# Attention output turned by float32 transposes and a 16-column product instead of one 144-column product

## The chip, the core and the metric

The kernel runs on one core of a Trainium2 chip. The metric is the device time of one execution in microseconds (us). TensorE (PE in the profile, with its weight loads as PEld) multiplies: it holds one operand as weights, up to 128 x 128, and streams the other past it, column by column. VectorE (DVE), ScalarE (ACT) and GpSimd (POOL) do the rest, SyncE (SP) issues most of the DMA transfers.

## The reference

Three stages follow each other: attention with a position bias, a layer of eight experts of which each token takes one, and a dense layer with a gate.

```python
scores = scale * np.matmul(q, k.transpose(0, 1, 3, 2)) + bias      # 4 batches, 8 heads, 576 tokens, 64 wide
attn = softmax(scores)                                             # divisor: sum + 1e-9
x = (attn @ v).transpose(0, 2, 1, 3).reshape(2304, 512)
logits = x @ w_gate + modality_bias[modality_id]                   # 8 experts
e_idx = argmax(logits);  gate_w = softmax(logits)[e_idx]
out[mask_e] = gate_w * (relu(x[mask_e] @ w1[e]) @ w2[e])           # e = 0..7
h = out @ w_in;  result = (h * sigmoid(1.702 * h)) @ w_out
```

The change lies at the end of attention, where `x` and its share of `logits` are made.

## The kernel before

Attention goes over 16 groups `g`: a pair of heads `hp` (4 of them) times a batch `b` (4). The 576 tokens of a group are four blocks of 128 rows and a last one of 64 rows; the last block holds both heads one above the other. That makes 80 units. A unit has its scores (`sc`, L571, float32r, 288 columns), which DVE joins with the bias (L574) and ACT exponentiates (L578). TensorE turns the result `p` by float32 transposes (`tp`, L599 and L612; `tp_r`, L607 and L618), ACT and DVE copy it out as `pt`.

Then comes the product with v (`pv`), in two parts for each group: part 0 has the first 256 tokens, part 1 the other 320 (256 and the last 64). Group 15 is cut into three, with part 2 of 256 and part 3 of the last 64 tokens alone. A part begins with one product in the form of the whole array (L646), after which each head has four products (L652) whose weights are 64 columns wide: head 0 in columns 0 to 63 of the array, head 1 in columns 64 to 127. The result has the head's width down the partitions and tokens along the row; ACT copies it to `xt` (L656).

`xs()` makes from it tokens down the partitions. The weights are 128 tokens of `xt`, and what streams past is `rh`, 144 columns: for each of the two heads 64 columns of the identity matrix and 8 columns of `w_gate`. So one product gives the turned x and the logits together (L673). For the last 64 tokens of a group the weights have 64 columns (L676). A float32 product that isn't a transpose shows in the trace as two passes, each with its own weight load; a transpose as one. DVE divides by the row sums: `Lp` (L692) takes the logits, `xo` (L708, L714) the x, and SP stores `xo` to `X`.

The kernel's text is not the order in which the engines work: a scheduler arranges the instructions of each engine as the program is built, and TensorE runs its products in the order written there. How many transposes, score products and pieces of `pv` stand beside each other is decided by it. After attention come the routing (a serial chain over DVE and TensorE), the experts and the dense layer.

Of the kernel before, what the change touches and what calls it, by code (L numbers as in the profile page):

```python
# [15 lines left out]
ALU = mybir.AluOpType  # L16
# [3 lines left out]
B, H, S, D = 4, 8, 576, 64  # L20
HP = H // 2
FH = 32
E, DM, FE = 8, 512, 1024
# [22 lines left out]
REST = (12, 12, 17, 17)  # L46
# [67 lines left out]
def body(ctx, tc, qk, vv, few, mid, ew1, ew2, ww, cst, alog, out, dbg=None):  # L114
    nc = tc.nc
    pe, act, dve, pool, sp = nc.tensor, nc.scalar, nc.vector, nc.gpsimd, nc.sync
    stop = dbg["stop"] if dbg else None

    biasD = tc.dram_tile([36 * TROWS + IROW], F32, name="biasD")
    X = dbg["X"] if dbg and "X" in dbg else tc.dram_tile([NT, DM], F32, name="X")  # L120
# [19 lines left out]
    ident = cs[:, C_ID:C_ID + 128]  # L140
# [149 lines left out]
    def top_expert(c):  # L290

        mx, dl, sc, m2 = (V[n][:, c] for n in ("mx", "dl", "sc", "m2"))
        n = c.stop - c.start
        dve.tensor_reduce(mx, Lacc[:, c], axis=AX.X, op=ALU.max)
        dve.tensor_tensor(dl, Lacc[:, c], mx[:, :, None].to_broadcast([128, n, E]), op=ALU.subtract)
        dve.scalar_tensor_tensor(sc, in0=dl, scalar=0.0, in1=cc(C_REV, E)[:, None, :].to_broadcast([128, n, E]),
                                 op0=ALU.is_ge, op1=ALU.mult)
        dve.tensor_reduce(m2, sc, axis=AX.X, op=ALU.max)
        return dve.tensor_tensor(V["A"][:, :, c].rearrange("p e c -> p c e"), sc,
                                 m2[:, :, None].to_broadcast([128, n, E]), op=ALU.is_equal)  # L300
# [150 lines left out]
    def attention():  # L451
# [28 lines left out]
        Lp = kp.tile([128, NTILE, 2, E], F32, name="Lp")  # L480
# [103 lines left out]
        def tps(i):  # L584
# [36 lines left out]
            if c == 1:  # L621
                todo.extend(pv_pieces(g, 0))
            if c == 3 and g == 15:
                *pv, _, G["xs"] = pv_pieces(g, 2)
                todo.extend(pv)
            if c == 4:
                if g == 15:
                    *pv, _, xs = pv_pieces(g, 3)
                    todo.extend(pv + [G["xs"], xs])
                else:  # L630
                    todo.extend(pv_pieces(g, 1))

        def pv_pieces(g, part):


            G = grp[g]
            hp, b = divmod(g, B)
            half = min(part, 1)
            main, tail = part < 3, part in (1, 3)
            cols = slice(0 if main else 256, 320 if tail else 256)  # L640
            W = cols.stop - cols.start

            def rest():
                G["ps", part] = (pst if part == 3 else psv).tile([128, 512], F32, tag="t" if part == 3 else "pv",
                                                                 name=f"pv{g}_{part}")
                pe.matmul(G["ps", part][:, :W], lhsT=vm[g][:, 512:640], rhs=G["pt", half][:, 8, cols],  # L646
                          start=True, stop=False)

            def pair(cc):
                ps = G["ps", part]  # L650
                for h in range(2):
                    pe.matmul(ps[64 * h:64 * h + 64, :W], lhsT=vm[g][:, 256 * h + 64 * cc:256 * h + 64 * cc + 64],  # L652
                              rhs=G["pt", half][:, 4 * h + cc, cols], start=False, stop=cc == 3)
                if cc == 3:
                    xt = G["xt", part] = p2.tile([128, 320], F32, tag="xt", name=f"xt{g}_{part}")[:, :W]
                    act.copy(xt, ps[:, :W])  # L656
                    ri = G["ri", part] = p2.tile([128, 3, 2], F32, tag=f"ri{half}", name=f"ri{g}_{part}")
                    if main:
                        dve.tensor_scalar_add(ri[:, 0:2], G["rs", 2 * half], 1e-9)
                    if tail:  # L660
                        pool.memset(ri[64:128, 2, :], 1.0)
                        for h in range(2):
                            dve.tensor_scalar_add(ri[0:64, 2, h:h + 1], G["rs", 4][64 * h:64 * h + 64], 1e-9)
                    used = ri[:, 0 if main else 2:3 if tail else 2]
                    dve.reciprocal(used, used)

            def xs():
                ps = (pst if part == 3 else psx).tile([128, 512], F32, tag="t" if part == 3 else "x", name=f"x{g}_{part}")
                xt, ri = G["xt", part], G["ri", part]
                rh = RH[:, hp]  # L670
                if main:
                    for c in range(2):
                        pe.matmul(ps[:, 144 * c:144 * c + 144], lhsT=xt[:, 128 * c:128 * c + 128], rhs=rh,  # L673
                                  start=True, stop=True)
                if tail:
                    pe.matmul(ps[:64, 288:432], lhsT=xt[:, W - 64:W], rhs=rh, start=True, stop=True)  # L676
                xo = p2.tile([128, 2 + half, 2, D], F32, tag=f"xo{half}", name=f"xo{g}_{part}")
                c1 = MAIN[b] + 2 * half

                shares = []  # L680
                if main:
                    shares.append((slice(0, 128), slice(c1, c1 + 2), ps[:, :288], ri[:, 0:2]))
                if tail:
                    shares.append((slice(64 * (b % 2), 64 * (b % 2) + 64), slice(REST[b], REST[b] + 1), ps[:64, 288:432],
                                   ri[:64, 2:3]))
                views = []
                for rows, cl, p_, r_ in shares:
                    n = 2 * (cl.stop - cl.start)
                    v_ = p_.rearrange("p (a n) -> p a n", n=72)
                    r_ = r_.rearrange("p c h -> p (c h)")[:, :, None]  # L690
                    views.append((v_, r_, n))
                    dve.tensor_tensor(Lp[rows, cl].rearrange("p c h e -> p (c h) e"), v_[:, :, 64:72],  # L692
                                      r_.to_broadcast([v_.shape[0], n, E]), op=ALU.mult)
                top = None
                if hp == HP - 1:

                    for h in range(2):
                        for rows, cl, _, _ in shares:
                            dve.tensor_tensor(Lacc[rows, cl], Lacc[rows, cl], Lp[rows, cl, h, :], op=ALU.add)
                    if tail and b >= 2:  # L700
                        top = top_expert(slice(0, NCA) if b == 2 else slice(NCA, NTILE))

                def store():
                    cols_ = slice(128 * hp, 128 * hp + 128)
                    r0 = b * S + 256 * half
                    if main:
                        v_, r_, n = views[0]
                        dve.tensor_tensor(xo[:, 0:2].rearrange("p c h d -> p (c h) d"), v_[:, :, :64],  # L708
                                          r_.to_broadcast([128, 4, 64]), op=ALU.mult)
                        sp.dma_start(X[r0:r0 + 256, cols_].rearrange("(c p) d -> p c d", p=128),  # L710
                                     xo[:, 0:2].rearrange("p c h d -> p c (h d)"))
                    if tail:
                        v_, r_, n = views[-1]
                        dve.tensor_tensor(xo[:64, 2], v_[:, :, :64], r_.to_broadcast([64, 2, 64]), op=ALU.mult)  # L714
                        sp.dma_start(X[b * S + 512:(b + 1) * S, cols_], xo[:64, 2].rearrange("p h d -> p (h d)"))
                if part == 2:
                    G["store"] = store
                else:
                    with tc.issue_after(top.ins) if top else ExitStack():
                        store()  # L720
                        if part == 3:
                            G["store"]()
                if tail and b == B - 1 and hp < HP - 1:
                    for h in range(2):
                        dve.tensor_tensor(Lacc, Lacc, Lp[:, :, h, :], op=ALU.add)
                if tail:
                    grp.pop(g)
            return [rest] + [lambda cc=cc: pair(cc) for cc in range(4)] + [lambda: None, xs]

        load_qkv(1)  # L730
# [403 lines left out]
```

## Time and profile before

| | |
|---|---|
| time, median of 3 runs | 1052.22 us (1052.21 to 1054.89) |
| the profiled execution's own time | 1050.38 us |
| its span, first to last instruction | 1048.7 us |
| mean granted TensorE clock | 0.988 |
| PE, busy share of the span | 95% (1001.1 us) |
| DVE, busy share of the span | 72% (750.3 us) |
| ACT, busy share of the span | 61% (639.2 us) |
| L673 on PE: 128 passes, busy | 21.6 us |
| L676 on PE: 32 passes, busy | 7.3 us |

The x products end at 352.6 us of the span; the routing follows, the experts take the time to 634 us and the dense layer the rest. The durations of single matmuls overlap: a pass of L673 lasts 289 ns in the records, and the next one starts 0.12 us after it. What a pass costs TensorE is therefore the distance from one start to the next. Where rows of the timeline merge n instructions, that distance is the merged time less the duration of one, divided by n - 1.

### The profile page before, as it was taken

The numbers are of one execution on the slowest core, as the hardware profiler recorded it, in microseconds if no ns is written. First come the engines' busy times: TensorE is split into PE (matmuls) and PEld (weight loads), VectorE is DVE, ScalarE is ACT, GpSimd is POOL, SyncE is SP. The second block draws the span as 40 slices with busy tenths as digits, with TensorE's granted clock in tenths as the row PEclk, the third lists the DMA queues.
The fourth block names the chain that finished last, engine by engine and source line by source line (L and its number), as shares of the span: only waits on it lengthen the run. The fifth ranks groups of instructions, "written<-read, shape, count | busy, mean of one in ns | idle before, by whom it ended". The sixth has DMA issues, their size and how long they took to land. (4 is left out here: it accounts for less than half of the span.)

```text
span 1048.7 us, 16882 instructions
## 1 busy us (share of the span) xinstructions
PE 1001.1 (95%) x5806; PEld 817.7 (78%) x5806; DVE 750.3 (72%) x1476; ACT 639.2 (61%) x1203; POOL 134.8 (13%) x136
## 2 busy tenths in 40 slices
PE   5699999999999589999999999999999999999997
PEld 1246777777777378888888888999989999999996
DVE  7886878787888799999999984735574666364433
ACT  7776777677777479999999973544442333232221
POOL 6410000000000245551111000000000000001212
PEclk9999999999999799999999999999999999999999
DMA  8977766776852331511261342400120111010111
GB/s 244 310 228 213 206 169 171 196 200 173 199 151 55 98 142 44 208 41 43 86 235 61 109 154 83 141 31 23 59 81 1 41 61 61 1 41 31 51 41 60
DMA packets 52057, 119.02 MB, mean 113 GB/s; under 512 B 8448, under 2 KB 17920, under 8 KB 51968
## 3 DMA queue, kind: packets, MB, share of 16 engines
q1 hardware_dynamic: 47024, 101.88, 33.0%
q0 software_dynamic: 4800, 15.73, 4.2%
q8 instruction: 47, 0.77, 0.3%
q14 instruction: 42, 0.34, 0.1%
q10 hardware_dynamic: 144, 0.29, 0.1%
HBM read 146.57 MB, written 25.84 MB: 164 GB/s over the span
## 5 line engine op out<-in xcount | busy, mean ns | idle before, releaser
L836 DVE TENSOR_TENSOR wl<-wraw,wh 128x1024 fp32r<-128x1024 f32 x167 | 198.9, 1245 | 6.4 <-ACT wh L834 4.5
L834 ACT CAST wh<-wraw 128x1024 fp32r<-128x1024 f32 x168 | 171.6, 1064 | 18.2 <-PE p L861 8.4
L1027 ACT ACTIVATE sg<-f 128x384 f32<-128x384 f32 x96 | 47.2, 492 | 177.5 <-PE f L1024 177.5
L1029 DVE TENSOR_TENSOR gg<-f,sg 128x384 f32<-128x384 f32 x96 | 53.4, 556 | 139.8 <-ACT sg L1027 139.7
L574 DVE CUSTOM_DVE_ANT_0 p<-sc,bias 128x576 f32<-128x576 f32 x144 | 106.9, 753 | 39.7 <-PE sc L571 38.8
L1024 PE MATMUL f<-yh,wh 128*128 128x384 f32 x384 | 129.9, 338 | 1.0 <-ACTq L976 1.0
L1024 PE MATMUL f<-yh,wl 128*128 128x384 f32 x384 | 129.5, 337 | 0.0
L1024 PE MATMUL f<-yl,wh 128*128 128x384 f32 x384 | 129.5, 337 | 0.0
L578 ACT ACTIVATE p<-p,mx 128x576 f32<-128x576 f32 x144 | 111.4, 774 | 14.2 <-DVE mx L574 11.0
L1057 PE MATMUL o<-wh,gl 128*128 128x512 f32 x288 | 114.0, 396 | 0.0
L1057 PE MATMUL o<-wl,gh 128*128 128x512 f32 x288 | 113.4, 394 | 0.0
L1057 PE MATMUL o<-wh,gh 128*128 128x512 f32 x288 | 113.4, 394 | 0.0
L571 PE MATMUL sc<-kk,qh 128*128 128x288 f32 x320 | 101.4, 334 | 2.9 <-ACT bev L253 2.1
L571 PE MATMUL sc<-kk,ql 128*128 128x288 f32 x320 | 88.9, 296 | 0.0
L1032 ACT CAST gh<-gg 128x384 fp32r<-128x384 f32 x96 | 49.3, 513 | 53.1 <-DVE gg L1029 52.8
L652 PE MATMUL pv<-pt,v 128*64 128x256 f32 (+2 forms) x528 | 77.5, 411 | 0.0
L1024 PEld LDWEIGHTS f<-yh,wh 128*128 128x128 f32 x384 | 72.1, 188 | 5.2 <-ACTq L976 1.4
L1033 DVE TENSOR_TENSOR gl<-gg,gh 128x384 fp32r<-128x384 f32 x96 | 53.5, 558 | 30.8 <-ACT gh L1032 30.8
L1024 PEld LDWEIGHTS f<-yl,wh 128*128 128x128 f32 x384 | 72.1, 188 | 4.1
L599 PE MATMUL tp<-cs,p 128*128 128x128 f32 x512 | 74.9, 274 | 0.2
L1024 PEld LDWEIGHTS f<-yh,wl 128*128 128x128 f32 x384 | 72.1, 188 | 0.0
L571 PEld LDWEIGHTS sc<-kk,qh 128*128 128x128 f32 x320 | 63.0, 197 | 9.5 <-ACT bev L253 4.2
(178 smaller groups left out, 2016.7 us busy)
## 6 DMA issues: line engine op xcount, KB each, us to landing
wraw<-in_moe_w_dram SPq DMA_DIRECT2D x176, 512.0 KB
cvraw<-in_ww_dram SPq DMA_DIRECT2D x32, 512.0 KB
biasD<-bev SPq DMA_DIRECT2D x36, 295.5 KB
raw<-in_qk_dram SPq DMA_DIRECT2D x16, 640.0 KB
Yc<-y POOLq DMA_DIRECT2D x21, 256.0 KB, 2.4
v<-in_vv_dram SPq DMA_DIRECT2D x16, 320.0 KB
kk<-qh SPq DMA_DIRECT2D x16, 320.0 KB
kk<-ql SPq DMA_DIRECT2D x16, 320.0 KB
```

The costliest lines, as they stand in the source:

```text
L571: pe.matmul(ps[:, hf, :288], lhsT=l_, rhs=r_[:, 288 * hf:288 * hf + 288], start=n == 0, stop=n == len(terms) - 1)
L574: dve.tensor_tensor_reduce(out=pp.rearrange("p (a j) -> p a j", a=2), in0=ps[:, :, :288], in1=bt[:, h].rearrange("p (a j) -> p a j", a=2), ...
L578: act.activation(pp, pp, AF.Exp, bias=mx[:, h:h + 1], scale=-1.0, accum_out=rs[:, c % 2, h:h + 1] if c < 4 else rs)
L599: pe.transpose(ps[:, 128 * cc:128 * cc + 128], p[:, c0:c0 + 128], ident)
L652: pe.matmul(ps[64 * h:64 * h + 64, :W], lhsT=vm[g][:, 256 * h + 64 * cc:256 * h + 64 * cc + 64], rhs=G["pt", half][:, 4 * h + cc, cols], s ...
L834: act.copy(h, t)
L836: V["split"] = by.tensor_tensor(l, t, h.bitcast(F32), op=ALU.subtract).ins
L1024: pe.matmul(ps, lhsT=w[x_][:, 128 * k_:128 * k_ + 128], rhs=y_[:, k_, :], start=k_ == 0 and n_ == 0, stop=k_ == 3 and n_ == 2)
L1029: dve.tensor_tensor(gg, ps, sg, op=ALU.mult)
L1032: act.copy(gh, gg)
L1033: dve.tensor_tensor(gl, gg, gh.bitcast(F32), op=ALU.subtract)
L1057: pe.matmul(po[t_], lhsT=a_[:, sl_], rhs=b_, start=fc == 0 and n_ == 0, stop=fc == 3 and n_ == 2)
```

## The change

Each block of 128 tokens is turned by one float32 transpose (128 columns streamed) into columns 0 to 383 of the bank, and the logits come from a product of their own, with the same weights and only the 16 columns of `w_gate`, into columns 384 to 431. The last 64 tokens of a group are taken with the 64 tokens in front of them as a whole block of 128, and only partitions 64 to 127 of that are used, so that the divisors of these tokens move to partitions 64 to 127 as well. Part 3 of group 15, which has 64 tokens alone, keeps weights of 64 columns. DVE's operations, the stores and their sizes are the same; some read other columns and partitions.

```diff
+            last, idle = (slice(64, 128), slice(0, 64))[::1 if main else -1]
+
...
-                        pool.memset(ri[64:128, 2, :], 1.0)
+                        pool.memset(ri[idle, 2, :], 1.0)
                         for h in range(2):
-                            dve.tensor_scalar_add(ri[0:64, 2, h:h + 1], G["rs", 4][64 * h:64 * h + 64], 1e-9)
+                            dve.tensor_scalar_add(ri[last, 2, h:h + 1], G["rs", 4][64 * h:64 * h + 64], 1e-9)
...
+                turned = []
                 if main:
-                    for c in range(2):
-                        pe.matmul(ps[:, 144 * c:144 * c + 144], lhsT=xt[:, 128 * c:128 * c + 128], rhs=rh,
-                                  start=True, stop=True)
-                if tail:
-                    pe.matmul(ps[:64, 288:432], lhsT=xt[:, W - 64:W], rhs=rh, start=True, stop=True)
+                    turned += [(slice(0, 128), xt[:, 128 * c:128 * c + 128], c) for c in range(2)]
+                if tail and main:
+                    turned.append((slice(0, 128), xt[:, W - 128:], 2))
+                elif tail:
+                    turned.append((last, xt, 2))
+                for rows, x_, c in turned:
+                    pe.transpose(ps[rows, 128 * c:128 * c + 128], x_, ident)
+                for rows, x_, c in turned:
+                    pe.matmul(ps[rows, 384 + 16 * c:400 + 16 * c].rearrange("p (h e) -> p h e", h=2), lhsT=x_,
+                              rhs=rh.rearrange("p (h n) -> p h n", h=2)[:, :, 64:72], start=True, stop=True)
...
-                    shares.append((slice(0, 128), slice(c1, c1 + 2), ps[:, :288], ri[:, 0:2]))
+                    shares.append((slice(0, 128), slice(c1, c1 + 2), ps[:, :256], ps[:, 384:416],
+                                   ri[:, 0:2]))
                 if tail:
-                    shares.append((slice(64 * (b % 2), 64 * (b % 2) + 64), slice(REST[b], REST[b] + 1), ps[:64, 288:432],
-                                   ri[:64, 2:3]))
+                    shares.append((slice(64 * (b % 2), 64 * (b % 2) + 64), slice(REST[b], REST[b] + 1), ps[last, 256:384],
+                                   ps[last, 416:432], ri[last, 2:3]))
                 views = []
...
-                    v_ = p_.rearrange("p (a n) -> p a n", n=72)
+                    v_ = p_.rearrange("p (a n) -> p a n", n=64)
                     r_ = r_.rearrange("p c h -> p (c h)")[:, :, None]
                     views.append((v_, r_, n))
-                    dve.tensor_tensor(Lp[rows, cl].rearrange("p c h e -> p (c h) e"), v_[:, :, 64:72],
+                    dve.tensor_tensor(Lp[rows, cl].rearrange("p c h e -> p (c h) e"), l_.rearrange("p (a e) -> p a e", e=E),
                                       r_.to_broadcast([v_.shape[0], n, E]), op=ALU.mult)
...
-                        dve.tensor_tensor(xo[:, 0:2].rearrange("p c h d -> p (c h) d"), v_[:, :, :64],
+                        dve.tensor_tensor(xo[:, 0:2].rearrange("p c h d -> p (c h) d"), v_,
...
-                        dve.tensor_tensor(xo[:64, 2], v_[:, :, :64], r_.to_broadcast([64, 2, 64]), op=ALU.mult)
-                        sp.dma_start(X[b * S + 512:(b + 1) * S, cols_], xo[:64, 2].rearrange("p h d -> p (h d)"))
+                        dve.tensor_tensor(xo[last, 2], v_, r_.to_broadcast([64, 2, 64]), op=ALU.mult)
+                        sp.dma_start(X[b * S + 512:(b + 1) * S, cols_], xo[last, 2].rearrange("p h d -> p (h d)"))
```

The scheduler arranges the new program anew. Three places on TensorE follow; `sc` are scores, `tp` and `tp_r` transposes of p, `pv` the product with v, `x` the block that is changed; the number at the end is the columns streamed, in front of it the weights' columns, and xN counts instructions in a row (numbers inside names are buffers).

First place, TensorE, the end of part 1 in a group in the middle of attention (group 6); before and now:

```order
L599 MATMUL tp_1_2533<-cs,p_2409 128x128 x4
L673 MATMUL x_1_2539<-rhw,xt_1_2489 128x144 x2
L676 MATMUL x_1_2539<-rhw,xt_1_2489 64x144
L646 MATMUL pv_0_2550<-pt_0_2419,v_2096 128x256
L652 MATMUL pv_0_2550<-pt_0_2419,v_2096 64x256 x2
L607 MATMUL tp_r<-cs,p_2409 128x128
```

```order
L599 MATMUL tp_1_2565<-cs,p_2441 128x128 x4
L681 MATMUL x_1_2571<-cs,xt_1_2521 128x128 x3
L683 MATMUL x_1_2571<-rhw,xt_1_2521 128x16 x3
L648 MATMUL pv_0_2585<-pt_0_2451,v_2121 128x256
L654 MATMUL pv_0_2585<-pt_0_2451,v_2121 64x256 x2
L607 MATMUL tp_r<-cs,p_2441 128x128
```

The surroundings stay; two products of 144 columns and one with narrow weights have become three transposes and three short products.

Second place, TensorE, a little later, where part 0 of group 7 ends; before and now:

```order
L652 MATMUL pv_0_2550<-pt_0_2419,v_2096 64x256 x6
L607 MATMUL tp_r<-cs,p_2457 128x128
L612 MATMUL tp_0_2615<-cs,p_2509 128x128 x4
L571 MATMUL sc_0_2566<-kk_2504,ql_2452 128x288
L571 MATMUL sc_0_2566<-kk_2504,qh_2406 128x288
L571 MATMUL sc_0_2566<-kk_2504,ql_2452 128x288
L571 MATMUL sc_1_2579<-kk_2504,ql_2452 128x288
L571 MATMUL sc_1_2579<-kk_2504,qh_2406 128x288
L571 MATMUL sc_1_2579<-kk_2504,ql_2452 128x288
L618 MATMUL tp_r<-cs,p_2509 64x128
L673 MATMUL x_0_2633<-rhw,xt_0_2598 128x144 x2
```

```order
L654 MATMUL pv_0_2585<-pt_0_2451,v_2121 64x256 x5
L571 MATMUL sc_0_2601<-kk_2536,qh_2438 128x288
L571 MATMUL sc_1_2614<-kk_2536,qh_2438 128x288
L654 MATMUL pv_0_2585<-pt_0_2451,v_2121 64x256
L607 MATMUL tp_r<-cs,p_2489 128x128
L612 MATMUL tp_0_2650<-cs,p_2541 128x128 x4
L681 MATMUL x_0_2668<-cs,xt_0_2633 128x128
L618 MATMUL tp_r<-cs,p_2541 64x128
L681 MATMUL x_0_2668<-cs,xt_0_2633 128x128
L683 MATMUL x_0_2668<-rhw,xt_0_2633 128x16 x2
L648 MATMUL pv_1_2712<-pt_1_2555,v_2121 128x320
L654 MATMUL pv_1_2712<-pt_1_2555,v_2121 64x320 x3
```

The six products of pv in a row are cut into five and one, and the next part of pv begins right behind x, before the scores that stood there.

Third place, TensorE, the pv products of part 1 that follow; before and now:

```order
L599 MATMUL tp_1_2669<-cs,p_2563 128x128 x3
L646 MATMUL pv_1_2675<-pt_1_2523,v_2096 128x320
L652 MATMUL pv_1_2675<-pt_1_2523,v_2096 64x320 x4
L607 MATMUL tp_r<-cs,p_2563 128x128
L571 MATMUL sc_0_2689<-kk_2504,qh_2406 128x288
```

```order
L571 MATMUL sc_1_2614<-kk_2536,ql_2484 128x288
L654 MATMUL pv_1_2712<-pt_1_2555,v_2121 64x320 x2
L571 MATMUL sc_0_2643<-kk_2536,qh_2438 128x288
L571 MATMUL sc_0_2643<-kk_2536,ql_2484 128x288
L571 MATMUL sc_0_2643<-kk_2536,qh_2438 128x288
L571 MATMUL sc_0_2643<-kk_2536,ql_2484 128x288
L654 MATMUL pv_1_2712<-pt_1_2555,v_2121 64x320 x2
```

The eight products of this part stood as four and four; now they stand as three, two, two and one, with scores between them. Over the whole of attention the products with 64-column weights of L652 form 64 runs before and, as L654, 74 now; runs of an odd number are 6 before (all of 256 columns) and 18 now (10 of 256 and 8 of 320 columns). All new cuts stand in the products of groups 7, 9 and 11; in the other groups from 4 on the order is as at the first place.

## Rows read from the trace of the kernel before

**Rows 1.** Stretches: us, busy us (count) PE, PEld, DVE, ACT, POOL; granted clock, DMA
```profile
120.00:180.00 60.00, 60.00 (x433) 45.72 (x431) 46.25 (x137) 43.36 (x108) 1.48 (x10) 1.00 0.65 171
...
240.00:300.00 60.00, 60.00 (x437) 46.26 (x436) 48.34 (x142) 45.18 (x113) 0.28 (x3) 1.00 0.74 190
...
352.00:360.00 8.00, 1.30 (x10) 0.61 (x10) 7.03 (x35) 3.21 (x9) 1.32 (x2) 0.65 0.07 20
```

**Rows 2.** Who waited for whom, 60 to 356 us: sum, times, longest (us)
```profile
DVE p L574 <- PE sc L571: 38.8, 56, 3.8
ACT pt L602 <- PE tp L599: 21.0, 34, 1.2
```

**Rows 3.** Timeline of PE around an x block of part 1: start, merged duration (us)
```profile
253.02 1.03 PE L599 MATMUL tp<-cs,p 128*128 128x128 f32 x8
253.89 0.66 PE L673 MATMUL x<-rhw,xt 128*128 128x144 f32 x4
254.48 0.46 PE L676 MATMUL x<-rhw,xt 128*64 128x144 f32 x2
254.87 0.70 PE L646 MATMUL pv<-pt,v 128*128 128x256 f32 x2
255.49 0.65 PE L652 MATMUL pv<-pt,v 128*64 128x256 f32 x4
256.08 0.33 PE L607 MATMUL tp_r<-cs,p 128*128 128x128 f32 x1
```

**Rows 4.** Timeline of the weight loads in the same stretch
```profile
253.78 0.55 PEld L673 LDWEIGHTS x<-rhw,xt 128*128 128x128 f32 x4
...
254.86 0.30 PEld L646 LDWEIGHTS pv<-pt,v 128*128 128x128 f32 x2 [0.20 <-issue]
```

**Rows 5.** Groups to 460 us: count | busy us, mean ns of one | idle before
```profile
L599 PE MATMUL tp<-cs,p 128*128 128x128 f32 x512 | 74.9, 274 | 0.2
L599 PEld LDWEIGHTS tp<-cs,p 128*128 128x128 f32 x512 | 60.8, 140 | 4.7 <-ACT p L578 2.4 <-issue 1.3 <-ACT pt L608 0.5
L673 PE MATMUL x<-rhw,xt 128*128 128x144 f32 x128 | 21.6, 289 | 0.5 <-ACT xt L656 0.5
L646 PEld LDWEIGHTS pv<-pt,v 128*128 128x128 f32 x66 | 10.0, 189 | 3.3 <-issue 2.8 <-ACT pt L608 0.5
L339 PEld LDWEIGHTS <-r_R 128*128 128x128 f16 x36 | 2.0, 103 | 6.1 <-DVE r_u L334 4.6 <-ACT r_R L309 0.5 <-DVE xl L856 0.4
```

**Rows 6.** Timeline of PE: runs of L652 of eight and of six passes
```profile
102.36 1.08 PE L652 MATMUL pv<-pt,v 128*64 128x256 f32 x8
103.37 0.33 PE L607 MATMUL tp_r<-cs,p 128*128 128x128 f32 x1
103.63 1.08 PE L652 MATMUL pv<-pt,v 128*64 128x256 f32 x6
104.64 0.40 PE L571 MATMUL sc<-kk,qh 128*128 128x288 f32 x1
```

**Rows 7.** Timeline of PE: a run of L652 with 320 columns
```profile
250.57 1.30 PE L652 MATMUL pv<-pt,v 128*64 128x320 f32 x8
251.80 0.33 PE L607 MATMUL tp_r<-cs,p 128*128 128x128 f32 x1
```

**Rows 8.** Timeline of PE: two passes of 64 columns; the last x products
```profile
350.49 0.43 PE L646 MATMUL pv<-pt,v 128*128 128x64 f32 x2
350.85 0.69 PE L652 MATMUL pv<-pt,v 128*64 128x64 f32 x16
...
352.15 0.46 PE L676 MATMUL x<-rhw,xt 128*64 128x144 f32 x2
```

**Rows 9.** Timeline of the weight loads in the routing: three f16 loads in a row
```profile
359.92 0.16 PEld L339 LDWEIGHTS <-r_R 128*128 128x128 f16 x3
```

**Rows 10.** Timeline of PE: the one wait beside an x block
```profile
207.48 0.66 PE L673 MATMUL x<-rhw,xt 128*128 128x144 f32 x4
208.33 0.40 PE L571 MATMUL sc<-kk,qh 128*128 128x288 f32 x1 [0.19 <-DVE mx L574]
```

More of the change, by code (lines that the diff above doesn't have):

```diff
@@ L681, in xs @@
                 if main:
-                    shares.append((slice(0, 128), slice(c1, c1 + 2), ps[:, :288], ri[:, 0:2]))
+                    shares.append((slice(0, 128), slice(c1, c1 + 2), ps[:, :256], ps[:, 384:416],
+                                   ri[:, 0:2]))
                 if tail:
-                    shares.append((slice(64 * (b % 2), 64 * (b % 2) + 64), slice(REST[b], REST[b] + 1), ps[:64, 288:432],
-                                   ri[:64, 2:3]))
+                    shares.append((slice(64 * (b % 2), 64 * (b % 2) + 64), slice(REST[b], REST[b] + 1), ps[last, 256:384],
+                                   ps[last, 416:432], ri[last, 2:3]))
                 views = []
-                for rows, cl, p_, r_ in shares:
+                for rows, cl, p_, l_, r_ in shares:
                     n = 2 * (cl.stop - cl.start)
-                    v_ = p_.rearrange("p (a n) -> p a n", n=72)
+                    v_ = p_.rearrange("p (a n) -> p a n", n=64)
                     r_ = r_.rearrange("p c h -> p (c h)")[:, :, None]
                     views.append((v_, r_, n))
-                    dve.tensor_tensor(Lp[rows, cl].rearrange("p c h e -> p (c h) e"), v_[:, :, 64:72],
+                    dve.tensor_tensor(Lp[rows, cl].rearrange("p c h e -> p (c h) e"), l_.rearrange("p (a e) -> p a e", e=E),
                                       r_.to_broadcast([v_.shape[0], n, E]), op=ALU.mult)
@@ L697, in xs @@
                     for h in range(2):
-                        for rows, cl, _, _ in shares:
+                        for rows, cl, *_ in shares:
                             dve.tensor_tensor(Lacc[rows, cl], Lacc[rows, cl], Lp[rows, cl, h, :], op=ALU.add)
```

## The prediction

> **What bounds the kernel now.** I read first the stretches of attention: TensorE is busy for all of 60 us in 120 to 180 and in 240 to 300, at a granted clock of 1.00, while DVE and ACT have 12 to 17 us to spare in each [rows 1]. Then the waits: where engines wait in attention, DVE and ACT wait for TensorE, 38.8 us over scores and 21.0 us over transposes [rows 2]. So from 120 us at the latest to the end of the x products TensorE sets the pace, and what its queue gains or loses there comes out at the end, since routing, experts and dense layer only follow. Last I read the timeline around an x block, to get distances between starts instead of durations [rows 3, 4]; they are worked out with the single durations [rows 5].
>
> Transposes: eight in 1.03 us, one lasts 0.274, so (1.03 - 0.274) / 7 = 0.108 us each [rows 3, 5]. Passes of the 144-column product: (0.66 - 0.289) / 3 = 0.124, two for each block of 128, so 0.25 us a block [rows 3, 5]. A weight load of 128 float32 columns with no pass running beside it: two in 0.30 us, one lasts 0.189, so 0.11 from one to the next [rows 4, 5]. In L673 that is hidden under the pass before, which streams longer than the load.
>
> The last 64 tokens cost more than their size. The fourth pass of L673 begins at 253.89 + 3 x 0.124 = 254.26 and has streamed by 254.385; L676 begins only at 254.48 [rows 3]. Changing from weights of 128 columns to 64 makes TensorE run empty first: 0.09 us. Then a load of half the columns lies bare (0.055), two passes take 0.24, and before L646 at 254.87 it runs empty again (254.48 + 0.055 + 0.24 + 0.09 = 254.865, which agrees), after which its load of 0.11 lies bare. Together 0.59 us.
>
> **The change part by part.** *Whole blocks.* 17 parts without a tail and 15 with one have 2 blocks each, 64 in all. Removed: 0.25 us each. Added: a transpose, 0.108, and two passes of 16 columns. By the rate of the transposes (128 columns in 0.108) such a pass streams 0.014 us, far less than the load of 0.11 for the next one, which can start only when the pass has taken its own weights. So the distance is the load's, 0.11. No row shows 16 float32 columns; the nearest is L646 with 64 columns, where two passes take 0.36 us from 350.49 to 350.85: a bare load 0.11, a second load 0.11 with the first pass hidden beneath it, the last pass 0.053, running empty 0.09, sum 0.36 [rows 8]. With both loads hidden but the first it would be 0.31. I take 0.11. The other end is a load as in the routing, three f16 loads in 0.16 us with 0.103 for one, 0.03 apart [rows 9, 5]. A block now costs 0.108 + 0.22 = 0.328, so 64 x (0.328 - 0.248) = **+5.1 us**.
>
> The Trainium skill, in TensorE: Matmul & The Clock Gate, section Back-to-back issue gap, has a table in which a product of 1 to 64 columns takes about 60 cycles, an estimate of 0.025 us, and says beside it that in a stream of loads and products both set the spacing. By the table alone the 16-column passes would be almost free; the rows on L646 speak for the load. That is the third rival below.
>
> *Tails.* 15 of the 16 tails take the form of the whole array: 0.59 goes, 0.328 comes, 15 x -0.26 = **-3.9 us**. The last one, part 3 of group 15, keeps narrow weights and has a transpose and two short passes for two of 144 columns; between -0.1 and +0.1 us, taken as nothing.
>
> *Order.* L652 works on two halves of the array at once, one head in each. A run of six passes takes as long as one of eight: 104.64 - 103.63 = 1.01 and 103.37 - 102.36 = 1.01 [rows 6]. So a product without a partner costs as much as two with one: two steps instead of one each, and every odd run one step more than if it were paired. Eight passes are four steps plus the change of form at both ends (0.055 bare, 0.09 empty): (1.01 - 0.145) / 4 = 0.216; with 320 columns (251.80 - 250.57 - 0.145) / 4 = 0.27 [rows 6, 7]. Odd runs rise from 6 to 10 with 256 columns and from 0 to 8 with 320: 4 x 0.216 + 8 x 0.27 = **+3.0 us**. There are 74 runs instead of 64. Each new one brings the change into 64 columns, 0.145, and back, 0.09 and a bare load of 0.055 (half, if a transpose follows, whose load lasts 140 ns in the records where others last 189 [rows 5]) or 0.11 (if scores follow, which is so for 15 instead of 4): 10 x 0.29 + 11 x 0.055 = **+3.5 us**. If this order cost nothing at all, both terms would be 0; if TensorE's wait for DVE at an x block, 208.33 instead of 207.48 + 4 x 0.124 = 207.98, so 0.35 us [rows 10], came three times more in each of the three disturbed groups, it would cost 3.2 us on top. I take no more waits, since order before has such places as well.
>
> *Off TensorE.* DVE reads as many elements as before, and stores and divisors only move to other partitions; DVE's 12 us of slack in each 60 hide them [rows 1], and without that cover a stall of 0.1 us in 32 parts would be 3 us. Lp now waits for the last short pass; behind it on DVE stands xo, and only the store and POOL's memset wait for that, neither of which TensorE needs soon.
>
> Sum: 5.1 - 3.9 + 3.0 + 3.5 = +7.7 us. On the profiled execution, span 1048.7 and own time 1050.38, that makes 1058.1; the median of the runs stands 1.84 above it, so the time is 1052.2 + 7.7 = **1060 us**.
>
> **Rivals.** *Short loads.* The weights of the turned block might load as fast as a transpose's, whose record is 0.05 shorter. Only loads between short passes are bare anew, 3 for two blocks and 5 for three: (17 x 3 + 15 x 5) x 0.05 = 6.3 us less, 1053.6. For it: the same xt serves both; against it: L673 loads the same xt in 190 ns, as L646 does.
>
> *The order costs nothing.* 5.1 - 3.9 = +1.2, so 1053.4. For it: the products are the same; against it: the run of six that took as long as eight.
>
> *Faster.* Passes spaced by 0.03, as the f16 loads are, cost 126 x 0.08 = 10.1 us less than forecast; a scheduler that kept pairs together in time would spare the 6.5 of the order too. The place is the short passes; it decides from a spacing of about 0.07 us on: 7.7 - 10.1 - 6.5 = -8.9, so 1043.3. Against it: 0.36 us for L646's two passes.
>
> *More waits.* Scores held back and then bunched leave DVE and ACT without work and then TensorE without transposes: 1060 + 3.2 = 1063.2.
>
> *The clock.* In 352 to 360 us, where TensorE was busy for 1.30 of 8 us, the granted clock was 0.65 on average, part of it at 1.2 GHz instead of 2.4 [rows 1]. A fall like that in each of the three disturbed groups would cost 3 x 8 x 0.35 = 8.4 us: 1068.4. The Trainium skill, same page, Part 4: PE-mode transpose, says that transposes don't count as work for the clock, so more of them would endanger it; but the clock is 1.00 throughout 120 to 300 us, where eight transposes in a row are common [rows 1, 3].
>
> **How the numbers follow.** The forecast has 0.73, short loads 0.07, free order 0.06, faster 0.04, more waits 0.08, the clock 0.02. A measurement of this kernel can tell about 0.3% from no change, 3.2 us. Forecast, waits and clock are slower (0.83), short loads and free order lie within it (0.13), one case is faster (0.04). The forecast's own range is 1057 to 1063; taken wide enough for the two near rivals below and for more waits above, 1053.5 to 1064.
>
> **What would show it.** Right: L683's passes 0.11 us apart although each streams 16 columns; TensorE goes from L683 to L648 without running empty; L654 in groups 7, 9 and 11 in runs of one and three that take a step each for single products; clock 1.00; the last x pass about 7.7 us later, the stages behind it as long as before. Wrong: a spacing near 0.06 or 0.03; last x products that end within 3 us of 352.6 [rows 8]; a change that comes from the experts or the dense layer.

## The result, and the profile after

| | median | lowest to highest | runs |
|---|---|---|---|
| before | 1052.53 us | 1052.21 to 1054.89 | 4 |
| after | 1060.95 us | 1060.22 to 1062.36 | 4 |

The ratio is 1.0081, with a 95% interval of 1.0064 to 1.0097: 8.5 us slower, between 6.7 and 10.2. The forecast was 1060.

The profiled run of after is the longest of its four (1062.36 us, span 1060.7; the other spans are 1058.6 to 1059.4). Where its 12.0 us over before's span lie is read from two places, the first scores and the last x products. The timeline of PE, the first scores of before and then the two places in after (start, merged duration in us, instruction, count):

```profile
35.98 0.37 PE L571 MATMUL sc<-kk,qh 128*128 128x288 f32 x1
```

```profile
37.84 0.37 PE L571 MATMUL sc<-kk,qh 128*128 128x288 f32 x1 [0.60 <-PE bias L237]
...
363.00 0.29 PE L683 MATMUL x<-rhw,xt 128*64 128x16 f32 x2
```

So 1.9 us were lost ahead of the first changed instruction; over the twelve traces of this case the first scores begin anywhere from 35.6 to 37.8. The last x products stand at 363.00 instead of 352.15 [rows 8], 10.9 later, of which 9.0 arose between the two places. From there to the end of the span it is 697.7 us, against 696.6. The loss lies in attention.

The stretches of after, with columns as in [rows 1], and who waited for whom from 60 to 367 us (sum in us, times, longest):

```profile
120.00:180.00 60.00, 60.00 (x450) 47.27 (x449) 48.01 (x139) 43.83 (x109) 1.46 (x10) 1.00 0.62 165
240.00:300.00 60.00, 59.17 (x410) 43.78 (x409) 44.95 (x122) 40.16 (x101) 0.28 (x3) 1.00 0.73 199
```

```profile
DVE p L574 <- PE sc L571: 39.3, 60, 3.6
...
ACT pt L602 <- PE tp L599: 17.2, 29, 1.2
```

TensorE still sets the pace and its clock is 1.00 as in [rows 1, 2]; in 240 to 300 it is no longer busy throughout but misses 0.83 us. Two of its disturbed groups account for that (below).

An x block of part 1 in a group whose order is unchanged, on PE and on the weight loads, as in [rows 3, 4]:

```profile
260.33 1.03 PE L599 MATMUL tp<-cs,p 128*128 128x128 f32 x8
261.20 0.49 PE L681 MATMUL x<-cs,xt 128*128 128x128 f32 x3
261.53 0.74 PE L683 MATMUL x<-rhw,xt 128*128 128x16 f32 x6
262.12 0.68 PE L648 MATMUL pv<-pt,v 128*128 128x256 f32 x2
262.73 0.65 PE L654 MATMUL pv<-pt,v 128*64 128x256 f32 x4
263.31 0.33 PE L607 MATMUL tp_r<-cs,p 128*128 128x128 f32 x1
```

```profile
261.09 0.36 PEld L681 LDWEIGHTS x<-cs,xt 128*128 128x128 f32 x3
261.42 0.75 PEld L683 LDWEIGHTS x<-rhw,xt 128*128 128x128 f32 x6
262.09 0.30 PEld L648 LDWEIGHTS pv<-pt,v 128*128 128x128 f32 x2
```

The loads of the short passes follow each other at (262.09 - 261.42) / 6 = 0.112 us, one unbroken row up to L648's, whose own load begins 0.112 after the last of L683. So the passes of 16 columns go at the loads' pace, and TensorE doesn't run empty between x and pv. (The starts of the passes themselves are a little closer in the records, 262.12 - 261.53 for six, because the first two stand close together.) From the first x pass to L607 it is 2.11 us, where before has 256.08 - 253.89 = 2.19 [rows 3].

The same engine in a disturbed group, the products of pv with weights of 64 columns:

```profile
254.11 0.75 PE L654 MATMUL pv<-pt,v 128*64 128x320 f32 x2
254.80 0.40 PE L571 MATMUL sc<-kk,qh 128*128 128x288 f32 x1
...
256.61 0.75 PE L654 MATMUL pv<-pt,v 128*64 128x320 f32 x2
257.29 0.66 PE L599 MATMUL tp<-cs,p 128*128 128x128 f32 x4
257.88 1.29 PE L654 MATMUL pv<-pt,v 128*64 128x320 f32 x6
259.10 0.33 PE L607 MATMUL tp_r<-cs,p 128*128 128x128 f32 x1
```

A product is two passes, so x2 is a single product and x6 are three. A single product takes 0.69 and 0.68 us. Three take 259.10 - 257.88 = 1.22, as much as four do before, 1.23 [rows 7]. The groups of instructions to 470 us (count | busy us, mean ns of one | idle before, and for whom), with L654 in place of L652 and L648 in place of L646:

```profile
L654 PE MATMUL pv<-pt,v 128*64 128x320 f32 x240 | 42.6, 447 | 0.0
L654 PE MATMUL pv<-pt,v 128*64 128x256 f32 x272 | 39.4, 392 | 0.0
...
L648 PE MATMUL pv<-pt,v 128*128 128x320 f32 x30 | 10.9, 444 | 1.3 <-DVE pt L620 1.3
```

One thing was not forecast, and it stands in the last row: L648 waits three times for DVE to copy the transposed rest of p, 1.3 us in all, which L646 of before does not do. Two of these waits are the 0.83 us that TensorE misses in 240 to 300, on its timeline:

```profile
247.68 0.81 PE L648 MATMUL pv<-pt,v 128*128 128x320 f32 x2 [0.35 <-DVE pt L620]
...
286.66 0.81 PE L648 MATMUL pv<-pt,v 128*128 128x320 f32 x2 [0.47 <-DVE pt L620]
```

### The profile page after: what moved, and what is told of

Its sections match the earlier page's. It is cut to its first block, busy times and chain, and to the rows that moved or that the text cites. A ratio compares the mean times of both kernels' runs of the same rounds, so it can differ in the third digit from the quotient of the medians.

```text
span 1060.7 us, 17032 instructions
## 1 busy us (share of the span) xinstructions
PE 1010.3 (95%) x5886; PEld 826.1 (78%) x5886; DVE 756.3 (71%) x1476; ACT 639.1 (60%) x1203; POOL 132.4 (12%) x136
## 5 line engine op out<-in xcount | busy, mean ns | idle before, releaser
L654 PE MATMUL pv<-pt,v 128*64 128x256 f32 (+2 forms) x528 | 82.7, 412 | 0.0
```

## The experiments

Two explanations were set against each other. By the first, the transposes and short products nearly pay for themselves with the tails, and the loss is the order: products of pv cut into more and odd runs in groups 7, 9 and 11. By its rival the x blocks themselves cost the 8.5 us and the order is harmless. Two edits that touch no x step give a frame in which the order of the 64-column products is 64 runs, 6 of them odd, with the old and the new x blocks alike:

```diff
-            t = bias[hp, c] = kp.tile([128, 2, S], F32, tag=f"bias{c}", name=f"bias{hp}_{c}")
+            t = bias[hp, c] = kp.tile([128, 2, S], F32, tag=f"bias{c}", bufs=2 if c < 1 else 1, name=f"bias{hp}_{c}")
...
-        starts = {2: 2, 4: 3, 12: 4, **{5 * g: g + 1 for g in range(B, 15)}}
+        starts = {2: 2, 4: 3, 12: 4, **{5 * g - 1: g + 1 for g in range(B, 15)}}
```

All results stand in one table. The ratio is to runs of before on the same chip, and the last column is (ratio - 1) x 1052. Differences between two rows are taken from that column, and their uncertainty from both intervals. Where busy times would count overlaps twice, distances are used: over TensorE's whole timeline from the first score to the last x product of a trace, the distance from each start to the next is added up, for each kind of instruction.

| kernel | runs of 64-column products, odd ones | median us | ratio, 95% interval | against before, us |
|---|---|---|---|---|
| after | 74, 18 | 1060.95 | 1.0081 (1.0064 to 1.0097) | +8.5 |
| e1_frame | 64, 6 | 1050.69 | 0.9986 (0.9974 to 0.9997) | -1.5 |
| e2_frame_tail | 64, 6 | 1045.19 | 0.9936 (0.9920 to 0.9951) | -6.7 |
| e3_frame_short | 64, 6 | 1052.32 | 1.0001 (0.9989 to 1.0012) | +0.1 |
| e4_frame_whole | 64, 6 | 1051.67 | 0.9995 (0.9985 to 1.0006) | -0.5 |
| e5_before_cut | 68, 12 | 1058.32 | 1.0060 (1.0044 to 1.0076) | +6.3 |
| e6_cols40 | 65, 8 | 1051.27 | 0.9997 (0.9988 to 1.0006) | -0.3 |
| e7_interleaved | 64, 6 | 1048.88 | 0.9969 (0.9959 to 0.9979) | -3.3 |
| e8_tail | 64, 6 | 1048.02 | 0.9961 (0.9948 to 0.9974) | -4.1 |
| e9_buffer_only | 67, 10 | 1054.82 | 1.0026 (1.0014 to 1.0039) | +2.7 |
| e10_start_only | 69, 12 | 1055.38 | 1.0026 (1.0017 to 1.0036) | +2.7 |

**The control, e1_frame**: before with the two edits above.

> The kernel before with two edits that touch no x step: a second buffer for the first of the two bias tiles, and the preparation of q and k of a later group one unit earlier. It is the control for the next three runs, which have the same two edits; in all four TensorE's row keeps the 64-column products of pv in 64 runs, 6 of them of odd length, as in the kernel before. Both theories: the products are the same and their order is nearly the same, so within 2 us of the kernel before, 1050 to 1053 us.

It came 1.5 us below before (uncertain by 1.2), within what was expected. So the frame may give a little by itself, and a difference between after and a kernel in the frame can hold that too.

**The whole change in that order, e4_frame_whole**: after with the two edits.

> The changed kernel with the same two edits as the control, by which its 64-column products of pv come back to 64 runs with 6 of odd length (74 runs with 18 of odd length in the changed kernel). Theory: the cut order of products in groups 7, 9 and 11 carries the loss (8.4 us in the trace of the changed kernel), so the time falls to the control's within 1.5 us, 1050 to 1053 us. Rival: the transposes and short products carry it, so the time stays 8 us above the control, at 1059 to 1061 us. The sizes of the prediction (blocks +5.1, tails -3.9, order +6.5) give 1.2 us above the control.

It is 0.9 us above the control (uncertain by 1.6) and 9.0 below after (by 2.1). The rival falls: the same transposes and short products, with the pv products in whole runs, cost nothing that can be measured. The groups of e4_frame_whole to 470 us:

```profile
L654 PE MATMUL pv<-pt,v 128*64 128x320 f32 x240 | 38.9, 445 | 0.0
L654 PE MATMUL pv<-pt,v 128*64 128x256 f32 x272 | 37.9, 391 | 0.0
...
L648 PE MATMUL pv<-pt,v 128*128 128x320 f32 x30 | 10.6, 434 | 0.0
```

Against the rows of after, the same 512 passes of L654 are busy for 5.2 us less; by distances, which leave out what overlaps, it is 4.4. L648's wait of 1.3 us is gone.

**Its two halves, e2_frame_tail and e3_frame_short.** The first keeps the 144-column product and changes the tail alone; the second has transposes and short products for the whole blocks and the old tail. Their core, against the control:

```diff
...
+                if tail and main:
+                    turned.append((slice(0, 128), xt[:, W - 128:], 2))
...
+                for rows, x_, c in turned:
+                    pe.matmul(ps[rows, 144 * c:144 * c + 144], lhsT=x_, rhs=rh, start=True, stop=True)
...
```

```diff
...
+                for rows, x_, c in turned:
+                    pe.transpose(ps[rows, 128 * c:128 * c + 128], x_, ident)
+                for rows, x_, c in turned:
+                    pe.matmul(ps[rows, 256 + 16 * c:272 + 16 * c].rearrange("p (h e) -> p h e", h=2), lhsT=x_,
+                              rhs=rh.rearrange("p (h n) -> p h n", h=2)[:, :, 64:72], start=True, stop=True)
+                for rows, x_ in tails:
+                    pe.matmul(ps[rows, 288:432], lhsT=x_, rhs=rh, start=True, stop=True)
...
```

> The control with only the last 64 tokens' part of the change: the 15 products on 64-column weights become products on 128-column weights (the 64 whole-array blocks keep the 144-column product, no transposes). If the tails cost what the prediction reads from the trace of before, 0.59 us of which 0.26 goes 15 times, 3.9 us below the control; to 5 us below it if the change of the weights' width costs the neighbouring passes too. The rival that the tails' time is hidden beside other engines' waits gives 0.

> The control with only the other part of the change: transposes and 16-column products for the 64 whole blocks, the tail's 144-column product on 64-column weights as before. By the prediction's term (loads pace the short passes, 0.328 against 0.248 us for a block) 64 x 0.08 = 5.1 us above the control. By the trace of the changed kernel, where the groups with an unchanged order of products come out even although the tails gain 3.9 us, 3.9 us above it. By the rival that the transposes and short products are themselves what makes the kernel 8.5 us slower and the order is harmless, 8.5 + 3.9 = 12 us above it. By the rival of short loads (a load of 16 columns' pass hidden in 0.055 us), 2 us below it.

The tail gave 5.2 us against the control (uncertain by 2.0), which is what the rows give for 144-column passes: a tail of 0.59 becomes two more passes of 0.124, 15 x -0.34 = -5.1. The timeline of PE in e2_frame_tail, part 1:

```profile
198.48 0.90 PE L681 MATMUL x<-rhw,xt 128*128 128x144 f32 x6
199.22 0.59 PE L648 MATMUL pv<-pt,v 128*128 128x256 f32 x2
199.74 0.65 PE L654 MATMUL pv<-pt,v 128*64 128x256 f32 x4
200.33 0.33 PE L607 MATMUL tp_r<-cs,p 128*128 128x128 f32 x1
```

From the first x pass to L607 it is 1.85 us, 0.34 less than in [rows 3]. The expectation of 3.9 had taken over the 0.328 of the short form.

The whole blocks cost 1.6 us (uncertain by 1.7), less than any theory but that of short loads, and 3.6 more than that one. In its trace the parts without a tail do cost what was forecast. Part 0 on PE, first in the control, then in e3_frame_short:

```profile
209.25 0.66 PE L673 MATMUL x<-rhw,xt 128*128 128x144 f32 x4
...
209.88 0.29 PE L571 MATMUL sc<-kk,ql 128*128 128x288 f32 x1
```

```profile
209.90 0.38 PE L681 MATMUL x<-cs,xt 128*128 128x128 f32 x2
210.12 0.52 PE L683 MATMUL x<-rhw,xt 128*128 128x16 f32 x4
...
210.70 0.29 PE L571 MATMUL sc<-kk,ql 128*128 128x288 f32 x1
```

To the second score it is 0.63 us and 0.80, so 0.17 for two blocks. The parts with the old tail go from 2.18 to 2.27, only 0.09 for two blocks: the last short pass streams a few columns before TensorE runs empty for the tail, where the old one streams 144. By these rows it would be 17 x 0.17 + 15 x 0.09 = 4.2. By distances, the x products of its trace take 3.5 us more than the control's, but L654 takes 0.5 less than its L652, because the control's 64 runs, 6 of them odd too, are not the same ones, and scores and transposes take 0.5 less. All kinds together it is 2.9 more, which the runs' 1.6 with its uncertainty allows.

**Before in a cut order, e5_before_cut**: the converse, old x blocks.

```diff
-        starts = {2: 2, 4: 3, 12: 4, **{5 * g: g + 1 for g in range(B, 15)}}
+        starts = {2: 2, 4: 3, 12: 4, **{5 * g + 1: g + 1 for g in range(B, 15)}}
```

> The kernel before with one edit that touches no x step: the preparation of q and k of the later groups starts two units later than in the control's frame (one later than before). Its x products are those of before, but TensorE's row now has the 64-column products of groups 7, 9 and 11 in pieces, as the changed kernel has: 68 runs, 12 of them odd, instead of 64 and 6. If the cut order alone costs time: by the prediction's prices 4 x 0.35 + 2 x 0.216 + 4 x 0.27 = 2.9 us above the kernel before; if each disturbed group costs what it cost in the changed kernel, 2.5 to 3.2 us, then 8 us above it. Rival (the order is harmless, only x's own form counts): 0 within 1.5 us.

6.3 us slower (4.6 to 8.0), without a change to x. That the order is harmless is refuted a second time; the price lies between the two that were expected. (All six added odd runs have 320 columns, so the prediction's prices give 4 x 0.35 + 6 x 0.27 = 3.0.) Its trace, 1055.0 us against 1048.7, is 6.3 longer as well: 4.8 of that lie between the first score and the last x product, and 1.6 behind them, where nothing was changed. The timeline of PE in a disturbed group, and the groups to 470 us:

```profile
250.16 1.29 PE L652 MATMUL pv<-pt,v 128*64 128x320 f32 x6
251.38 0.33 PE L607 MATMUL tp_r<-cs,p 128*128 128x128 f32 x1
...
253.58 1.30 PE L652 MATMUL pv<-pt,v 128*64 128x320 f32 x8
254.80 0.33 PE L607 MATMUL tp_r<-cs,p 128*128 128x128 f32 x1
```

```profile
L652 PE MATMUL pv<-pt,v 128*64 128x320 f32 x240 | 41.4, 446 | 0.0
...
L646 PE MATMUL pv<-pt,v 128*128 128x320 f32 x30 | 10.8, 440 | 1.0 <-DVE pt L620 1.0
```

Three products and four take the same 1.22 us within one trace. And the wait on DVE comes here too, 1.0 us, so it belongs to the order and not to the new x blocks.

**One frame edit at a time, e9_buffer_only and e10_start_only**: after with either line of the frame.

> The changed kernel with only one of the frame's two edits, the second buffer for the first bias tile: 67 runs of 64-column products, 10 of odd length (64 and 6 in e4_frame_whole, 74 and 18 in the changed kernel). If the cut order is the loss, the time lies in proportion between the two: 3/10 of the 9.3 us between them, 2.8 us above e4_frame_whole, 1054.5 us (2.0 us above it by the prediction's prices, 3 x 0.35 + 4 x 0.24). Rival: the frame's edits work by their transfers and not by the order, so that one of the two alone gives back all (1051.7 us) or nothing (1061 us).

> The changed kernel with only the other of the frame's two edits, the preparation of q and k one unit earlier: 69 runs of 64-column products, 12 of odd length. In proportion: 5/10 of 9.3 us, 4.7 us above e4_frame_whole, 1056.3 us (3.2 us above it by the prediction's prices, 5 x 0.35 + 6 x 0.24). Rival as in e9_buffer_only: all or nothing.

Both are 3.3 us above e4_frame_whole (uncertain by 1.7 and 1.5), where 2.8 and 4.7 were expected in proportion. Neither gives back all or nothing; as far as the intervals can tell, the loss goes with the cuts: 64, 67, 69 and 74 runs stand at -0.5, +2.7, +2.7 and +8.5 us. L648 waits for DVE in neither. Whether the frame's earlier transfers do something besides can't be told from these.

**What paces a short pass, e6_cols40 and e7_interleaved**, both on e4_frame_whole. The first streams 40 columns instead of 16, of which DVE reads the same 16:

```diff
-                    pe.matmul(ps[rows, 384 + 16 * c:400 + 16 * c].rearrange("p (h e) -> p h e", h=2), lhsT=x_,
-                              rhs=rh.rearrange("p (h n) -> p h n", h=2)[:, :, 64:72], start=True, stop=True)
+                    pe.matmul(ps[rows, 384 + 40 * c:424 + 40 * c].rearrange("p (h e) -> p h e", h=2), lhsT=x_,
+                              rhs=rh.rearrange("p (h n) -> p h n", h=2)[:, :, 52:72], start=True, stop=True)
...
```

The second puts each product in front of its own transpose:

```diff
                 for rows, x_, c in turned:
-                    pe.transpose(ps[rows, 128 * c:128 * c + 128], x_, ident)
-                for rows, x_, c in turned:
                     pe.matmul(ps[rows, 384 + 16 * c:400 + 16 * c].rearrange("p (h e) -> p h e", h=2), lhsT=x_,
                               rhs=rh.rearrange("p (h n) -> p h n", h=2)[:, :, 64:72], start=True, stop=True)
+                    pe.transpose(ps[rows, 128 * c:128 * c + 128], x_, ident)
```

> The changed kernel in the control's frame (as the run e4_frame_whole) with 40 columns instead of 16 in every short product; the 24 added columns are computed and not used. If the loads of the weights set the pace of the short passes (0.11 us each in the trace of the changed kernel), 24 more columns hide below them: within 1 us of e4_frame_whole, but its row has one run of 64-column products more and two more of odd length, for which 0.9 us is to be taken off. If the columns set the pace, 158 passes by 24 columns at two cycles of 2.4 GHz, 0.02 us each, make 3.2 us more.

> The changed kernel in the control's frame with each block's short product ahead of its own transpose (product, transpose, product, transpose), instead of all transposes and then all products; the order of the 64-column products is that of e4_frame_whole. If loads set the short passes' pace, the load of the pass behind each transpose now hides below the transpose's 0.108 us, and only one pass in two stays bare: 0.27 instead of 0.328 us for a block, 79 x 0.05 = 4 us below e4_frame_whole. If the passes cost their 0.11 us for another reason than the load (a fixed time of each pass), nothing is saved: within 1 us of e4_frame_whole.

The timeline of PE, part 1: first e4_frame_whole, then e6_cols40, then e7_interleaved.

```profile
201.16 0.49 PE L681 MATMUL x<-cs,xt 128*128 128x128 f32 x3
201.49 0.74 PE L683 MATMUL x<-rhw,xt 128*128 128x16 f32 x6
...
203.27 0.33 PE L607 MATMUL tp_r<-cs,p 128*128 128x128 f32 x1
```

```profile
200.27 0.49 PE L681 MATMUL x<-cs,xt 128*128 128x128 f32 x3
200.60 0.76 PE L683 MATMUL x<-rhw,xt 128*128 128x40 f32 x6
...
202.38 0.33 PE L607 MATMUL tp_r<-cs,p 128*128 128x128 f32 x1
```

```profile
200.63 0.29 PE L681 MATMUL x<-rhw,xt 128*128 128x16 f32 x2
200.78 0.31 PE L683 MATMUL x<-cs,xt 128*128 128x128 f32 x1
200.92 0.29 PE L681 MATMUL x<-rhw,xt 128*128 128x16 f32 x2
...
202.60 0.33 PE L607 MATMUL tp_r<-cs,p 128*128 128x128 f32 x1
```

With 40 columns the stretch from the first x pass to L607 takes the same 2.11 us, and the kernel the same time within 1.5 us; by columns (24 more at the transposes' 0.108 / 128 us, 158 times) it would have been 3.2 slower. Interleaved, the stretch is 1.97 and from one product to the next it is 200.92 - 200.63 = 0.29 instead of 0.328, and the kernel is 2.7 us faster (uncertain by 1.5), of 4 expected. The load sets the pace, and a transpose between two products hides part of one. The Trainium skill, in TensorE: Matmul & The Clock Gate, section LDWEIGHTS (loading the stationary operand), prices a load by its columns alone, an estimate of 0.107 us for 128; the 0.112 of the loads here is 5% above it.

**The tail alone, e8_tail**: the tail's diff of e2_frame_tail on before, without the frame.

> The tail's part of the change alone, on the kernel before without the frame's two edits (144-column products kept for all blocks, no transposes; the order of the 64-column products stays in 64 runs with 6 odd). The same 3.9 to 5.5 us as between e2_frame_tail and e1_frame: 1047 to 1048.5 us. If the gain of e2_frame_tail hung on the frame's earlier transfers, it shrinks below 2 us: 1050.5 or more.

4.1 us below before (uncertain by 1.4), so the tail's gain doesn't hang on the frame. With the frame, e2_frame_tail is the fastest of all, 0.9936 of before (0.9920 to 0.9951), below both before and after.

## Why the prediction held, and which step failed

*What bounds the kernel*: right. The loss arose on TensorE in attention at a clock of 1.00, and the stages behind it took as long as before to about 1 us.

*Whole blocks, +5.1, and tails, -3.9*: their sum in the kernel as changed, +1.2, was measured by e4_frame_whole against its control as +0.9, uncertain by 1.6. Singly, the pace of 0.11 was right, to 0.112 by the loads. A part without a tail costs 0.17 more where 2 x 0.08 was forecast, a part with one 0.07 to 0.08 less where 0.16 - 0.26 = -0.10 was. So the rival of short loads fell by rows and by e6_cols40. The table that the prediction weighed, in the Trainium skill, TensorE: Matmul & The Clock Gate, section Back-to-back issue gap, an estimate of 0.025 us for so few columns, was not the pace of these passes, which have new weights of 128 columns each: 0.112.

*Order, +6.5*: right in its mechanism and, by the traces, in its size. The price of a single product was exact: a change of form of 0.145 and two steps of 0.27 make 0.685, and the records say 0.69 and 0.68. The forecast's 6.5 divides into what lies inside the runs, 3.0 + 10 x 0.145 = 4.45, and what lies on the scores and transposes around them, 10 x 0.145 + 11 x 0.055 = 2.05. By distances, before to after, L654 takes 4.45 us more than L652, and scores and transposes of p 1.71 more, 6.2 together. The price inside the runs holds for the other cuts too: 6 x 0.27 + 4 x 0.145 = 2.2 us against 2.2 by distances in e5_before_cut, 4 x 0.216 + 3 x 0.145 = 1.3 against 1.3 in e9_buffer_only, 2 x 0.216 + 4 x 0.27 + 5 x 0.145 = 2.2 against 2.2 in e10_start_only (the first compared with before, the others with e4_frame_whole).

By times the order's share is less sharp. The 9.0 between after and e4_frame_whole, uncertain by 2.1, is more than 6.5 and 1.3 of waits, but it holds what the frame does too; if that is the 1.5 of e1_frame, 7.5 are left, uncertain by 2.4. In e5_before_cut attention is 4.8 longer in its trace, of which 1.0 are waits, so 3.8 stand against the 3.0 of the prices. The 3.3 of e9_buffer_only, where the prices give 3 x 0.35 + 4 x 0.216 = 1.9, and the 3.3 of e10_start_only, where they give 5 x 0.35 + 2 x 0.216 + 4 x 0.27 = 3.3, agree with them within their uncertainty. That the surroundings of a cut cost more than was priced is therefore not shown.

*No more waits*: this is the step that failed. Three waits came, 1.3 us, less than half of the 3.2 that the rival gave. The place was another, too: not DVE's maxima at an x block, but DVE's copy of the transposed rest of p (L620), which the next part of pv needs. In the order's second place that part begins right behind x, where scores had stood and had covered the copy. The rest is transposed just before (L618), and L648 comes only after the copy, at 247.68. From L618 to the start of that part it is 1.2 us in each of the three disturbed groups, and at least 2.5 us in every group of before. The timeline of after, PE and DVE:

```profile
246.46 0.30 PE L618 MATMUL tp_r<-cs,p 128*64 128x128 f32 x1
...
247.41 0.22 DVE L620 COPY pt<-tp_r 64x64 f32<-64x64 f32 x1
```

The reason that was given, that order before has such places as well, does not carry. A part of 320 columns begins right behind x three times in after and waits each time, and twice with the same wait in e5_before_cut; in e4_frame_whole, e9_buffer_only and e10_start_only it never begins there. Before has one such place, without a wait, but there the rest was transposed long ahead; its timeline of PE:

```profile
106.93 0.27 PE L618 MATMUL tp_r<-cs,p 128*64 128x128 f32 x1
...
111.26 0.66 PE L673 MATMUL x<-rhw,xt 128*128 128x144 f32 x4
111.75 0.70 PE L646 MATMUL pv<-pt,v 128*128 128x320 f32 x2
```

With the waits the account closes: 7.7 + 1.3 = 9.0 us, where the distances of the two traces differ by 8.9 and the times by 8.5. The missed term is small, so the time stayed inside the range.

*Off TensorE, the clock*: nothing came from either; the granted clock of after is 1.00 in every stretch from 120 to 361 us, the disturbed groups among them.

What stays open is why the scheduler, given the new x blocks, cuts three groups. Two edits far from x undo it.

## What to carry to other kernels

Where a scheduler arranges the instructions, a change is two changes, and the second can be the larger: compare the old and the new order on the bounding engine, count what stands apart that stood together, and price each cut from runs of odd length in the trace of before. To learn what an edit is worth by itself, find neutral edits that bring the order back and time it in that frame. Passes of few columns with new weights each cost the load of these weights here, so there was nothing to gain by shortening a pass below it.

## What the runs showed of the hardware beyond that

- Loads of 128 float32 columns follow each other at 0.112 us whether 16 or 40 columns stream between them; a transpose, 0.108, put between two short products hides part of one.
- Products whose weights take one half of the array's columns went two at a time only in pairs: with 320 columns a single one took 0.69 us, three 1.22 and four 1.22.
- TensorE waited for DVE's copy where the order put a pv part right behind x, with new and old x blocks alike (1.3 us in after, 1.0 in e5_before_cut), although DVE is busy for only 45 of 60 us around it in after. The cuts of e9_buffer_only and e10_start_only, which have no such place, brought no such wait.
